# Block-sparse attention and SwiGLU: another order for GpSimd's gathers and copies in the sparse steps

## The chip, the cores and the metric

One core of one Trainium2 chip runs the whole program. The metric is device time in microseconds (us). Engines are named as the profile names them: PE (TensorE, matrix multiply), DVE (VectorE), ACT (ScalarE), POOL (GpSimd), SP (SyncE, which here only issues DMAs). Each engine executes its own instructions strictly in the order of the program and waits on semaphores for the others. DMAs started by POOL are issued by instructions that stand in POOL's own queue.

## The reference, cut to what matters

```python
batch, n_heads, seq, head_dim = (4, 8, 768, 64)      # block 32: 24 blocks of queries and of keys
scores = scale * np.matmul(q, k.transpose(0, 1, 3, 2))
mask = np.abs(blk_i - blk_j) <= 1
mask = mask | (blk_i == 0) | (blk_j == 0) | (blk_i == n_blocks - 1) | (blk_j == n_blocks - 1)
for qb in range(n_blocks):
    for kb in sampled_blocks[qb]:                    # 3 random key blocks for each query block
        mask[qb * block:(qb + 1) * block, kb * block:(kb + 1) * block] = True
attn = softmax(np.where(mask, scores, -1e9));  attn_out = np.matmul(attn, v)

x = attn_out.transpose(0, 2, 1, 3).reshape(B * S, H * D)          # 3072 tokens x 512
xn = x / np.sqrt(np.mean(x * x, axis=-1, keepdims=True) + 1e-06) * rms_g
g = xn @ w_gate                                                    # 512 x 1536
out = (g * sigmoid(g) * (xn @ w_val)) @ w_out                      # 1536 x 512
```

A query block looks at its three neighbours, the first and the last block, and three sampled blocks; the first and last query blocks look at everything.

## The kernel before, in words

**Stages.** Batch 0 is computed densely, with the mask added through extra rows of the operands (lines 926 to 1054). Batches 1 to 3 are computed sparsely, in 18 *chunks* of four query blocks (128 queries): in each batch five chunks of neighbouring blocks and one *edge* chunk (blocks 0, 23, 1, 22). In the order of work the edge chunks are numbers 5, 11 and 16. The feed-forward part (FFN) of finished tokens is cut into small pieces (`gate`, `val` and `down`, lines 730 to 786) that are fed into PE between the pieces of attention.

**Sparse steps.** The loop at line 1078 runs steps i = 0 to 18. Each step has ten *positions*. Work is put under a position with `do(n, f)`; at line 1159 the loop goes through the positions in order, runs everything put there, in the order in which it was put, and then lets `position()` add FFN pieces. This is the order of the program, hence of each engine's queue; no scheduler moves anything afterwards. Step i does the following.

- `values(i - 1, 0)` and `values(i - 1, 1)` at positions 0 and 1 (line 634): PE multiplies the probabilities of chunk i-1 with its values, 64 small matmuls for an ordinary chunk and 128 for an edge chunk (L644).
- `normalise` (L669, L670 on DVE), `squares(i - 1)` at position 4 (L677 on ACT), `rms_power(i - 1)` at position 5 (two tiny POOL instructions, L681 and L682) and `x_scaled(i - 1)` at position 7 (L698 or L695 on DVE). For most chunks the scaled rows `xs` are then transposed by a DMA that SP issues (L700) into `xg`, which the FFN reads; for chunks 4, 8, 16 and 17 (`by_pe`) PE transposes them a step later.
- `scores(i, part)` from position 1 on (L620 on PE, the exponential L628 on ACT). An ordinary chunk has four parts, an edge chunk eight.
- preparation for later chunks; nx is i + 1. The keys of chunk nx are collected in `kg` (two buffers in turn): neighbours and edges by DVE (`gather_k`, L471 and L476), sampled blocks by ACT and POOL (`sampled_k`, L485): of the three sampled blocks of a query block ACT copies two and POOL one, so POOL makes four copies for an ordinary chunk and two for an edge chunk. The values of a chunk are collected in `vg` (three buffers in turn) by indirect DMAs from a table in DRAM (`gather_v`, L512), one for each query block. An ordinary chunk has four of them, an edge chunk two, for its third and fourth block; `gather_v` skips the blocks 0 and 23, so that its call for the first two of an edge chunk issues nothing.
- keys and queries of the next batch but one are loaded (`load_kq`, L126, two POOL DMAs with a cast to bf16 on the way), values of it (`load_v`, by SP), and keys and queries of the next batch are transposed by PE (`turn`, L455) into the tables `KT` and `QN`. `table(b)` (L446) writes the table of values of a batch to DRAM, one POOL DMA, at position 0 of steps 4 and 10.

**POOL's queue around the change.** In step i the queue of POOL holds, in this order: at position 0 the copies of sampled keys of chunk nx (in step 0: at position 6); at 1 and 2 the third and fourth gather of chunk nx; at 5 `rms_power`; at 6 and 7 the first and second gather of chunk nx + 1 (at 8 and 9 where nx + 1 is the first chunk of a batch); at 9, in steps 4 to 7, `load_kq` for one pair of heads of batch 3. The variable `at` (line 1124) is 6 in step 0 and 0 in all others; it also places the copies of DVE and ACT.

Buffers bind as follows. The gathers of chunk c write `vgs[c % 3]`, which `values(c - 3)` reads last. The copies of chunk c write `kgs[c % 2]`, which `scores(c - 2)` reads last. `turn` of batch 3 reads what `load_kq` brought: keys at position 6 and queries at position 9 of steps 7 to 10. FFN groups enter at position 4 of the step two after their last chunk (line 1065): chunks 0 and 1 in step 3, chunks 2 to 4 in step 6, 5 to 8 in step 10, 9 to 12 in step 14, 13 to 15 in step 17.

Of the kernel before, what the change touches and what calls it, by code (L numbers as in the profile page):

```python
# [18 lines left out]
def kernel(  # L19
# [57 lines left out]
    PB = NCH // (B - 1)  # L77
    sizes = [2, 3, 4, 4, 3, 2]
    assert sum(sizes) == NCH
    sgroups, at = [], 0  # L80
# [384 lines left out]
    def gather_k(i, copy):  # L465
        b, qbs = chunks[i]
        kg, src = kgs[i % 2], KT[b % 2]
        j0 = 2 if qbs[0] == 0 else 0
        n = QB - j0
        step = (qbs[j0 + 1] - qbs[j0]) * HB  # L470
        yield lambda: copy(  # L471
            out=kg[:, :, j0:QB, W0:W0 + 3 * HB],
            in_=spaced(src[:, :, (qbs[j0] - 1) * HB:(qbs[j0] + 2) * HB], step, n, 3 * HB))
        if i % PB < 2:
            for to, at in ((F0, 0), (L0, NT - HB)):
                yield lambda to=to, at=at: copy(  # L476
                    out=kg[:, :, :, to:to + HB],
                    in_=src[:, :, at:at + HB].unsqueeze(2).to_broadcast([P, H, QB, HB]))

    def sampled_k(i, on):  # L480
        b, qbs = chunks[i]

        def one(j, r):
            copy = act if by_act(qbs[j], r) else pool
            copy(out=kgs[i % 2][:, :, j, R0 + r * HB:R0 + (r + 1) * HB],  # L485
                 in_=KT[b % 2][:, :, bass.ds(kat[(qbs[j], r)], HB)])

        return [lambda j=j, r=r: one(j, r) for j in range(QB) if qbs[j] not in (0, NB - 1)
                for r in range(NRND) if by_act(qbs[j], r) == (on == "act")]

    def gather_q(i, copy):
        b, qbs = chunks[i]
        runs = [(0, QB)] if qbs[0] else [(0, 2), (2, QB)]
        for lo, hi in runs:
            for a in range(2):
                for w in range(2):
                    rows = QN[b % 2][w * D:(w + 1) * D]
                    to = Qd[i % 2][a * D:(a + 1) * D, :, a, w, lo * HB:hi * HB]
                    if qbs[0]:
                        yield lambda to=to, rows=rows: copy(  # L500
                            out=to, in_=rows[:, :, qbs[0] * HB:(qbs[0] + QB) * HB])
                    else:
                        yield lambda to=to, rows=rows, lo=lo, hi=hi: copy(
                            out=to.rearrange("p h (j s) -> p h j s", j=hi - lo),
                            in_=spaced(rows[:, :, qbs[lo] * HB:(qbs[lo] + 1) * HB],
                                       (qbs[lo + 1] - qbs[lo]) * HB, hi - lo, HB))

    def gather_v(i, js=range(QB)):
        b, qbs = chunks[i]
        for j in js:  # L510
            if qbs[j] not in (0, NB - 1):
                nc.gpsimd.indirect_dma_start(  # L512
                    vgs[i % 3][:, j, :], None, vtab[b][:],
                    bass.IndirectOffsetOnAxis(ap=vidx[:, qbs[j]:qbs[j] + 1], axis=0))
# [563 lines left out]
    for i in range(NCH + 1):  # L1078
        jobs = {}

        def do(n, f):
            jobs.setdefault(n, []).append(f)
# [3 lines left out]
        nx = i + 1 if i + 1 < NCH else None  # L1086
# [36 lines left out]
        if nx is not None:  # L1123
            at = 6 if nx == 1 else 0
            gk, gq = list(gather_k(nx, dve)), list(gather_q(nx, dve))
            if at == 0:
                for m, x in enumerate(gq):
                    do(3 + m * 2 // len(gq) * 2, x)
                do(4, gk[0])
                for x in gk[1:]:  # L1130
                    do(6, x)
            else:
                do(at, gk[0])
                for m, x in enumerate(gk[1:]):
                    do(at + 1 + m, x)
                for m, x in enumerate(gq):
                    do(at + 1 + m // 2, x)
            kact, kpool = sampled_k(nx, "act"), sampled_k(nx, "pool")
            for x in kpool:
                do(at, x)  # L1140
            for m, x in enumerate(kact):
                do(at + (m + 1) * (NPOS - 1 - at) // len(kact), x)
            if nx > 1:
                do(1, lambda: gather_v(nx, (2,)))
                do(2, lambda: gather_v(nx, (3,)))
            if nx + 1 < NCH:
                at = 6 if (nx + 1) % PB else 8
                do(at, lambda: gather_v(nx + 1, (0,)))
                do(at + 1, lambda: gather_v(nx + 1, (1,)))
        for m in range(min(6, len(by_need)) if i < 2 else 0):  # L1150
            do(m, next_address)

        bl, sl = divmod(i + 2, PB)
        if 0 < bl and bl + 2 < B and sl < NP:
            do(9, lambda: load_kq(bl + 2, sl))
        bv, sv = divmod(i + 3, PB)
# [44 lines left out]
```

## Time and profile before

| what | value |
|---|---|
| time, median of 3 runs | 309.54 us (309.53 to 310.64) |
| the profiled execution's own time | 309.54 us |
| its span, first to last instruction of the program | 307.8 us |
| mean granted TensorE clock | 0.994 |
| PE busy | 284.4 us, 92% |
| DVE, ACT, POOL busy | 215.2, 198.9, 147.1 us |
| sparse steps | from about 75 us to the end |

What lies between the span and the time (1.7 us) is start and end of the execution. The views used below are the profile's page (busy time of the engines, costliest groups), the table of waits (who waited for whom, total in us, times, longest), the chain of work that ended last, and the timeline of single engines. In a timeline row the columns are the start, the duration, the engine, the line, the operation and its tiles, the count, and in brackets the idle time before it with what ended it. A wait put down to "issue" ended with nothing that the profile shows.

### The profile page before, as it was taken

To read this page: it belongs to the slowest core of one execution; us is meant where nothing else is said; L and a number is where in the kernel's file an instruction comes from. 1 tells how busy PE (TensorE), PEld (TensorE's weight loads), DVE (VectorE), ACT (ScalarE), POOL (GpSimd) and SP (SyncE) were. 2 spreads that over 40 slices of the span, in tenths; PEclk is the share of its full clock that TensorE was granted. 3 is DMA by queue.
4 is the path that set the end of the run, shared out by engine and by line. 5 is a ranking of instruction groups with operands and counts; after the bars stand their busy time and mean duration, and the time that the engine had idled before them with its cause. 6 is when DMAs were issued, how large, how long until landed. Compare 5 with 4: busy or idle time off the path is not lost.

```text
span 307.8 us, 9872 instructions
## 1 busy us (share of the span) xinstructions
PE 284.4 (92%) x3871; PEld 187.8 (61%) x3871; DVE 215.2 (70%) x596; ACT 198.9 (65%) x467; POOL 147.1 (48%) x244
## 2 busy tenths in 40 slices
PE   7899999978969889998899898899999999999995
PEld 6677885767548657765566454454445455555683
DVE  7888798667847757963999377877449991396480
ACT  4896775666738787876898786662675575633331
POOL 9858243582746364884887542816550710000000
PEclk9999999999989999999999999999999999999999
DMA  7999999999663287598997654415543233100202
GB/s 137 290 208 201 207 227 281 257 298 227 133 200 86 76 205 267 105 250 227 141 250 205 202 163 116 119 44 148 157 156 87 78 83 100 58 2 0 104 1 68
DMA packets 37426, 47.44 MB, mean 154 GB/s; under 512 B 11184, under 2 KB 29380, under 8 KB 37380
## 3 DMA queue, kind: packets, MB, share of 16 engines
q0 software_dynamic: 21184, 32.60, 48.3%
q1 hardware_dynamic: 16132, 14.18, 15.9%
q8 instruction: 30, 0.49, 0.6%
q14 instruction: 16, 0.13, 0.2%
q10 hardware_dynamic: 64, 0.03, 0.0%
HBM read 46.45 MB, written 8.83 MB: 180 GB/s over the span
## 4 chain that ended last, share of the span: by engine, by line
PE 77%; DMA 8%; DVE 5%; issue 5%; POOL 2%; ACT 1%; ACTq 0%; DVEq 0%; POOLq 0%
PE gp L737 19%; PE vp L748 19%; PE yp L766 17%; PE st L620 7%; PE op L644 6%; DMA gain<-in_moe_rms_g_dram 4%; PE st L527 3%; PE tqk L455 2%; DMA kbf<-in_k_dram 2%; DMA xg<-xs 2%; PE op L536 2%; DVE u L752 1%; DVE hps L756 1%; DVE junk L570 1%; POOL kbf L126 1%
## 5 line engine op out<-in xcount | busy, mean ns | idle before, releaser
L737 PE MATMUL gp<-xg,wg 128*128 128x256 bf16 (+2 forms) x432 | 81.6, 309 | 2.3 <-ACT yo L771 1.1
L748 PE MATMUL vp<-xg,wv 128*128 128x256 bf16 (+2 forms) x432 | 81.3, 310 | 2.1 <-DVE u L752 1.2
L741 ACT ACTIVATE th<-gp 128x256 bf16<-128x256 f32 (+2 forms) x108 | 50.0, 463 | 44.0 <-PE gp L737 30.3
L512 POOL DMA_INDIRECT vg<-vtab,vidx x66 | 66.9, 1014 | 18.2 <-issue 13.6
L766 PE MATMUL yp<-wo,hps 128*128 128x512 bf16 (+1 forms) x300 | 72.0, 371 | 0.2 <-issue 0.2
L752 DVE SCALAR_TENSOR_TENSOR u<-th,gp 128x256 bf16<-128x256 bf16 (+2 forms) x108 | 54.5, 505 | 24.4 <-ACT th L741 20.9
L628 ACT ACTIVATE ex<-st 128x512 bf16<-128x512 f32 x84 | 50.4, 600 | 31.3 <-PE st L620 29.9
L756 DVE TENSOR_TENSOR hps<-u,vp 128x256 bf16<-128x256 bf16 (+2 forms) x108 | 55.1, 510 | 18.7 <-PE vp L748 3.3
L737 PEld LDWEIGHTS <-wg 128*128 128x128 bf16 x432 | 39.6, 98 | 20.5 <-issue 3.9
L748 PEld LDWEIGHTS <-wv 128*128 128x128 bf16 x432 | 39.6, 98 | 20.3 <-issue 3.4
L681 POOL TENSOR_TENSOR ssq<-ssq,eps 128x1 f32<-128x1 f32 x18 | 3.5, 195 | 86.6 <-ACT junk L677 86.5
L766 PEld LDWEIGHTS <-hps 128*128 128x128 bf16 x300 | 26.0, 98 | 20.9 <-issue 0.5
L530 ACT ACTIVATE ex<-st 128x768 bf16<-128x768 f32 x42 | 33.3, 813 | 5.3 <-PE st L527 4.9
L644 PEld LDWEIGHTS <-ex 128*32 128x32 bf16 x1344 | 16.2, 95 | 21.8 <-issue 20.1
L644 PE MATMUL op<-vg,ex 128*32 128x66 bf16 x1056 | 20.8, 196 | 7.1 <-issue 6.8
L771 ACT ACTIVATE yo<-yp 128x512 f32<-128x512 f32 (+1 forms) x25 | 14.6, 584 | 17.1 <-PE yp L766 16.8
L527 PE MATMUL st<-wide_q,wide_k 88*128 88x256 bf16 x144 | 23.0, 272 | 1.5 <-DVE wide_q L345 1.1
L669 DVE RECIPROCAL rz<-op 128x4 f32<-128x4 f32 x36 | 6.4, 177 | 15.4 <-PE op L644 9.7
L620 PE MATMUL st<-wide_q 128*128 128x64 bf16 x256 | 16.0, 197 | 0.6 <-issue 0.6
L620 PEld LDWEIGHTS <-wide_q 128*128 128x128 bf16 x256 | 12.9, 101 | 5.6 <-issue 0.8
L527 PEld LDWEIGHTS <-wide_k 88*128 88x128 bf16 x144 | 12.9, 97 | 5.3 <-DVE wide_q L345 2.0
L670 DVE TENSOR_TENSOR stage<-op,rz 128x256 bf16<-128x256 f32 x36 | 15.3, 425 | 1.2
(147 smaller groups left out, 385.4 us busy)
## 6 DMA issues: line engine op xcount, KB each, us to landing
out_dram<-yo SPq DMA_DIRECT2D x20, 256.0 KB
vraw<-in_v_dram SPq DMA_DIRECT2D x12, 384.0 KB
kbf<-in_k_dram POOLq DMA_DIRECT2D x15, 192.0 KB
vtab<-Vs POOLq DMA_DIRECT2D x3, 792.0 KB
qbf<-in_q_dram POOLq DMA_DIRECT2D x12, 192.0 KB
vraw<-in_v_dram POOLq DMA_DIRECT2D x4, 384.0 KB
wg<-in_moe_w_gate_dram POOLq DMA_DIRECT2D x4, 384.0 KB
wv<-in_moe_w_val_dram POOLq DMA_DIRECT2D x4, 384.0 KB
```

The costliest lines, as they stand in the source:

```text
L512: nc.gpsimd.indirect_dma_start(vgs[i % 3][:, j, :], None, vtab[b][:], bass.IndirectOffsetOnAxis(ap=vidx[:, qbs[j]:qbs[j] + 1], axis=0))
L527: nc.tensor.matmul(out=at[:, e], lhsT=KT0[0:KR, h, jt * P:(jt + 1) * P], rhs=QT0[0:KR, h, c0 * P:(c0 + 2) * P], start=True, stop=True)
L530: nc.scalar.activation(out=ex[:, 3 * part:3 * (part + 1), :], in_=at[:, 0:3], func=AF.Exp, scale=SCALE)
L620: nc.tensor.matmul(out=st[:, at:at + UN], lhsT=lhsT, rhs=Qd[i % 2][:, h, :, :, j * HB:(j + 1) * HB].rearrange("p a w s -> p (a w) s"), sta ...
L628: nc.scalar.activation(out=ex.rearrange("p (u s w) -> p u s w", s=HB, w=2), in_=st.rearrange("p (u w s) -> p u s w", s=HB, w=2), func=AF.E ...
L644: nc.tensor.matmul(out=op[j * BLK:(j + 1) * BLK, at:at + VW], lhsT=lhsT, rhs=rhs, start=(n == 0), stop=(n == of - 1))
L737: nc.tensor.matmul(out=gp[:, 0:tg], lhsT=wg[:, c, f * P:(f + 1) * P], rhs=xg[:, c, 0:tg], start=(c == 0), stop=(c == KD - 1))
L741: nc.scalar.activation(out=th[:, 0:tg], in_=gp[:, 0:tg], func=AF.Tanh, scale=0.5)
L748: nc.tensor.matmul(out=vp[:, 0:tg], lhsT=wv[:, c, f * P:(f + 1) * P], rhs=xg[:, c, 0:tg], start=(c == 0), stop=(c == KD - 1))
L752: nc.vector.scalar_tensor_tensor(out=u[:, 0:tg], in0=th[:, 0:tg], scalar=1.0, in1=gp[:, 0:tg], op0=ALU.add, op1=ALU.mult)
L756: nc.vector.tensor_tensor(out=hps[f][:, 0:tg], in0=u[:, 0:tg], in1=vp[:, 0:tg], op=ALU.mult)
L766: nc.tensor.matmul(out=yp, lhsT=hps[f][:, tt * P:(tt + 1) * P], rhs=wo[:, f, lo:hi], start=(f == 0), stop=(f == NF - 1))
```

## The change

In every step the copies of sampled keys by POOL go from position 0 to position 6, behind `rms_power`. The third and fourth gather of chunk nx go from positions 1 and 2 to 0 and 1. The first and second gather of chunk nx + 1 go from 6 and 7 to 2 and 3, ahead of `rms_power`; where nx + 1 begins a batch they stay at 8 and 9. The loads of keys and queries of batch 3 go from position 9 of steps 4 to 7 to position 9 of steps 5 to 8. Number, kind and size of all instructions stay as they were, and in the built program PE, DVE, ACT and SP have the same instructions in the same order as before.

```diff
             for x in kpool:
-                do(at, x)
+                do(6, x)
             for m, x in enumerate(kact):
                 do(at + (m + 1) * (NPOS - 1 - at) // len(kact), x)
             if nx > 1:
-                do(1, lambda: gather_v(nx, (2,)))
-                do(2, lambda: gather_v(nx, (3,)))
+                do(0, lambda: gather_v(nx, (2,)))
+                do(1, lambda: gather_v(nx, (3,)))
             if nx + 1 < NCH:
-                at = 6 if (nx + 1) % PB else 8
+                at = 2 if (nx + 1) % PB else 8
                 do(at, lambda: gather_v(nx + 1, (0,)))
                 do(at + 1, lambda: gather_v(nx + 1, (1,)))
...
-        bl, sl = divmod(i + 2, PB)
+        bl, sl = divmod(i + 1, PB)
         if 0 < bl and bl + 2 < B and sl < NP:
             do(9, lambda: load_kq(bl + 2, sl))
```

## The prediction

> **What bounds the kernel now.** I read the page first (busy shares, costliest groups), then the table of waits, then the timelines of POOL, PE and ACT in the steps where POOL has most to do, then the chain that ended last. From the page:
>
> ```profile
> span 307.8 us, 9872 instructions
> PE 284.4 (92%) x3871; PEld 187.8 (61%) x3871; DVE 215.2 (70%) x596; ACT 198.9 (65%) x467; POOL 147.1 (48%) x244
> ...
> PE 77%; DMA 8%; DVE 5%; issue 5%; POOL 2%; ACT 1%; ACTq 0%; DVEq 0%; POOLq 0%
> ...
> L512 POOL DMA_INDIRECT vg<-vtab,vidx x66 | 66.9, 1014 | 18.2 <-issue 13.6
> ...
> L681 POOL TENSOR_TENSOR ssq<-ssq,eps 128x1 f32<-128x1 f32 x18 | 3.5, 195 | 86.6 <-ACT junk L677 86.5
> ```
>
> PE is busy for 284.4 of 307.8 us, so that all its idle time together is 23.4 us, start and end of the kernel included. POOL is busy for under half of the span; most of its idle time, 86.5 us, it spends in front of the RMS power, waiting for ACT's squares. The change moves work of POOL alone, so it can only matter where somebody waits for POOL or for a DMA that POOL issues. From the table of waits (engine and line, whom it waited for, total us, times, longest):
>
> ```profile
> POOL ssq L681 <- ACT junk L677: 86.5, 15, 15.4
> DVE xs L698 <- POOL rstd L682: 2.1, 2, 2.0
> PE op L644 <- issue: 8.0, 16, 1.0
> DVE xs L695 <- POOL rstd L682: 1.5, 2, 1.2
> ...
> PE gp L737 <- DMA xg<-xs: 0.8, 1, 0.8
> ```
>
> Nobody waits for POOL's copies, PE hardly ever for a gather (0.4 us in all, by the answer on L644), and DVE four times for the RMS power, 3.6 us. But POOL was late itself in none of these four: L681 began 0.08 us after ACT had finished (chunk 8: ACT's accumulator ends at 170.76, L681 starts at 170.84). What remains for PE is 0.8 us on one transpose and 8.0 us of short gaps inside the small matmuls of `values`.
>
> Now POOL's timeline in its fullest stretch, steps 7 and 8, where the loads of batch 3 come on top:
>
> ```profile
> 152.99 0.18 POOL L681 TENSOR_TENSOR ssq<-ssq,eps 128x1 f32<-128x1 f32 x1
> 153.26 0.80 POOL L682 TENSOR_TENSOR rstd<-ssq,mhalf 128x1 f32<-128x1 f32 x1
> 154.23 1.00 POOL L512 DMA_INDIRECT vg<-vtab,vidx  x1 [0.17 <-issue]
> 155.54 0.96 POOL L512 DMA_INDIRECT vg<-vtab,vidx  x1 [0.30 <-issue]
> 156.50 0.80 POOL L126 DMA_DIRECT2D kbf<-in_k_dram  x1
> 157.26 0.81 POOL L126 DMA_DIRECT2D qbf<-in_q_dram  x1
> 157.99 1.06 POOL L485 COPY wide_q<-wide_k 128x128 bf16 x4
> 159.23 1.05 POOL L512 DMA_INDIRECT vg<-vtab,vidx  x1 [0.17 <-issue]
> 160.58 1.00 POOL L512 DMA_INDIRECT vg<-vtab,vidx  x1 [0.31 <-issue]
> 161.61 0.19 POOL L681 TENSOR_TENSOR ssq<-ssq,eps 128x1 f32<-128x1 f32 x1
> ```
>
> From one RMS power to the next are 8.62 us without a wait: RMS power 1.07, two gathers 2.44, two loads 1.49, four copies 1.06, two gathers 2.56. ACT's squares came at 152.91 and 161.53, also 8.62 us apart. POOL is exactly full here, and anything put ahead of the RMS power would show.
>
> **The change part by part.** It adds and removes no instruction. I place each moved one by adding these durations to the times at which the other engines were ready in the profiled execution, whose time, 309.54 us, equals the median.
>
> *Two gathers ahead of the RMS power, and a new wait.* The first two gathers of chunk i+2 now stand at positions 2 and 3 of step i, and write the buffer that `values(i-1)` has just read. POOL waits for PE's last matmul of `values(i-1)`, and the RMS power of chunk i-1 is queued behind that. That happens in ten steps. From the end of `values` to the end of ACT's accumulator there are 3.71 us (chunk 4: 128.11 to 131.82) to 6.22 us; the two gathers take 2.44. They fit where POOL stands ready when `values` ends. Where POOL is full it comes later, and the RMS power slips. For chunk 4: RMS power of chunk 3 ends at 124.64, two copies to 125.2, six gathers to 132.9 (`values(4)` ended at 128.11, no wait), L681 at 133.0 instead of 132.27, 0.7 us late; its reader `xs` began at 134.94 and the power would end at 133.9. For chunk 6: from 145.43, copies to 146.5, loads to 148.0, gathers to 150.5 and 153.0, L681 0.1 late. Chunk 7: 0.2 late. `xs` of these two began 2.47 and 2.23 us after the power. Cost 0; with that cover gone 1.0 us in all. In front of chunk 8's power, where DVE does wait, the two gathers would belong to edge chunk 11 and do not exist.
>
> *The copies behind the RMS power.* They become ready later by most of a step, and `scores` of chunk i+1 follow. For chunk 8, PE and ACT before:
>
> ```profile
> 156.47 1.05 PE L644 MATMUL op<-vg,ex 128*32 128x66 bf16 x64
> 157.45 0.41 PE L620 MATMUL st<-Qd,kg 128*128 128x64 bf16 x8
> ...
> 156.96 0.30 ACT L485 COPY kg<-wide_k 128x128 bf16 x1
> ```
>
> POOL's copies for it ended at 150.43, 7.0 us ahead of the scores. They would now end at 155.2, 2.2 us ahead, and ACT's last copy into the same tile (156.96 plus 0.30) comes later still. Worked out alike, the cover is 3.1 us for chunk 2, 2.0 for chunk 3, 2.2 for chunk 7, 1.8 for chunk 9 and more elsewhere. Cost 0.
>
> A rule speaks against this place: the Trainium skill, "SBUF — State Buffer", section "Who interferes with whom", says that a DVE instruction with two SBUF inputs and a GpSimd one that reads SBUF exclude each other. The copies now begin where DVE begins `xs`, which at L698 has two such inputs. The trace has such a meeting: copies at 97.23 took 1.52 us instead of 1.0, `xs` at 97.26 took 0.88 instead of 0.75. In the two steps with copies where DVE waits for the power at L698 (chunks 12 and 15) this is 0.13 each by the rows, 0.3 us on an engine with idle time: 0 in the sum, 0.3 its upper end. By the rule in full, DVE held for one whole copy (0.36, L485's longest group mean), it would be at most 0.7 us.
>
> *The other gathers* come about 3 us earlier and change nothing: `vg` had landed at least 8 us before its reader (chunk 8: last landing 156.96 by its semaphore, `values` at 165.01). In step 0 the first gather of chunk 2 passes two loads for batch 2, delayed by 1.3 us and not needed before 123 us. Cost 0.
>
> *The loads of batch 3* move from 127.1, 135.7, 147.9 and 156.5 to about 134.9, 146.5, 155.2 and 164. The longest landing that the trace gives for them is 8.3 us, the transposes on PE that read them start at 153.11, 161.65, 170.08 and 180.62: at least 5 us remain. SP's queue has none of this. Cost 0; with the cover gone PE would stand until the landing, up to 8 us.
>
> *DMA traffic beside the transpose of chunk 1.* The chain of work that ended last runs through it:
>
> ```profile
> 107.48 0.67 DVE xs L698
> ...
> 108.18 5.91 DMA xg<-xs
> 114.09 0.14 issue
> 114.22 0.60 PE gp L737 x4
> ```
>
> PE waits 0.8 us for it. Before, four gathers were issued between 106.3 and 112.6; now the copies come first, and two gathers follow from about 107.5, the other pair having gone out near 99. The wait can vanish (-0.8) or, if the transpose takes as long as the longest one (6.85 us, issued at 147.96 beside loads), grow by 0.9. With half as many gathers beside it I take half of the wait: -0.4. The Trainium skill, "DMA: Bandwidth & Descriptors", section "SWDGE vs HWDGE vs iDMA", says that an engine serves the queues of the two kinds of DMA in turn; by that alone halving the other side would take the whole wait, -0.8, sum 308.7. That the one transpose with no gather near it took 2.4 us (253.93) agrees.
>
> *The gaps in `values`.* Their cause is not in the trace: "issue". Those in the sparse steps come within some 2 us of a DMA issued by POOL, and `values` of chunks 14, 16 and 17, with none, have no gap; but chunks 7 and 8 have DMAs and no gap either. After the change the gathers still fall into or just ahead of most `values`; only chunk 11's (gaps of 0.32, 0.49 and 0.46) become free of them: -1.3 if gathers are the cause. At the other end, six chunks without gaps (1, 2, 7, 8, 12, 15) might get one of 0.5 each: +3.0. I take 0, because nearly every chunk keeps its neighbours.
>
> Sum: 309.54 - 0.4 = 309.1 us.
>
> **The rivals.** *Faster.* The transpose's wait goes and chunk 11's gaps go: 309.54 - 0.8 - 1.3 = 307.4 us. For it: the gaps stand beside gathers. Against: the clean chunks with gathers. *Slower.* PE releases the buffer later than its rows say, so the gathers reach POOL only with ACT's squares and stand whole in front of the RMS power. For it: DVE's reading of chunk 5's result waited until 140.47, though `values` ended at 138.47 by the rows. Against: most of DVE's readings show no such wait. With a lateness of 2.5 us copies miss their scores at chunks 3, 7, 8 and 9 by 0.5, 0.3, 0.3 and 0.7, and DVE, held at `xs` by up to 2.5 in the steps with chunks 12 and 14, passes on some 1.2: 309.5 + 3.0 = 312.5 us. It decides from about 1.8 us of lateness, the least cover. *The change does little of what it says.* Edge chunks and chunks that begin a batch have no gathers to move ahead; this ends where my forecast does.
>
> **How the numbers follow.** About 0.5% (1.5 us) can be told from no change. Within it 0.50: every step has a named cover of at least 1.0 us. Faster rival 0.26. Slower rival 0.24: the covers of copies shrink everywhere, and that of scores is 1.8 us at the least. The likeliest case gives 309.1, alone 307.9 to 311.0. The range goes from 306.9 (the faster rival with half a microsecond of gaps more) to 312.4, nearly the slower rival.
>
> **What would show it.** Right: L681 within 0.8 us of ACT's accumulator in each step; no wait of PE on POOL's copies before `scores`; POOL waiting for PE before gathers where it waited for ACT. Wrong: DVE waiting more than 3.6 us for L682; PE standing at L620 for L485 or at L455 for loads; the gaps at L644 far from 8.0 us.

## The result, and the profile after

The changed kernel takes 325.79 us (median of 6 runs, 324.20 to 326.87) beside 310.05 us of the kernel before (6 runs, 308.99 to 311.59): 1.0516 times as long, 95% interval 1.0478 to 1.0554. The forecast was 309.1 us, with a range up to 312.4. The kernel before itself takes 308.99 to 311.59 us in some sets of runs (a set is made on one chip) and 290.20 to 292.39 us in others, and the result above is from a set of the first kind. I call them *sets with gaps* and *sets without gaps*, for the reason that the trace gives.

The profiled execution of the changed kernel took 326.87 us. From its page:

```profile
span 325.1 us, 9900 instructions
...
PE 293.6 (90%) x3871; PEld 192.8 (59%) x3871; DVE 215.6 (66%) x596; ACT 199.9 (61%) x467; POOL 145.4 (45%) x244
...
PEclk9999999999979999599987999989999999999999
...
L512 POOL DMA_INDIRECT vg<-vtab,vidx x66 | 66.0, 1000 | 28.3 <-issue 12.2
...
L644 PE MATMUL op<-vg,ex 128*32 128x66 bf16 x1056 | 23.3, 197 | 15.0 <-issue 14.6
```

And from its table of waits (engine and line, whom it waited for, total us, times, longest):

```profile
POOL ssq L681 <- ACT junk L677: 89.3, 16, 15.4
...
PE op L644 <- issue: 15.8, 30, 1.2
...
POOL vg L512 <- PE op L644: 9.9, 8, 3.0
...
DVE xs L698 <- POOL rstd L682: 3.8, 2, 3.3
...
DVE xs L695 <- POOL rstd L682: 2.1, 2, 1.8
```

The span grew by 17.3 us (307.8 to 325.1). PE's busy time grew by 9.2 (284.4 to 293.6) and its idle time, span less busy, by 8.1 (23.4 to 31.5). Two readings fill this.

*Idle.* The gaps inside `values` (L644 by "issue") went from 8.0 us in 16 places to 15.8 in 30: 7.8 of the 8.1. Chunk 4 shows what one looks like. PE, with the matmuls of both halves of `values(4)` and the FFN between them:

```profile
127.15 0.43 PE L644 MATMUL op<-vg,ex 128*32 128x66 bf16 x32
127.51 0.73 PE L748 MATMUL vp<-xg,wv 128*128 128x256 bf16 x4
128.50 0.24 PE L644 MATMUL op<-vg,ex 128*32 128x66 bf16 x4 [0.26 <-ACT th L741]
129.21 0.26 PE L644 MATMUL op<-vg,ex 128*32 128x66 bf16 x4 [0.47 <-issue]
130.12 0.25 PE L644 MATMUL op<-vg,ex 128*32 128x66 bf16 x3 [0.66 <-issue]
130.87 0.21 PE L644 MATMUL op<-vg,ex 128*32 128x66 bf16 x2 [0.50 <-issue]
131.57 0.25 PE L644 MATMUL op<-vg,ex 128*32 128x66 bf16 x3 [0.49 <-issue]
132.28 0.43 PE L644 MATMUL op<-vg,ex 128*32 128x66 bf16 x16 [0.45 <-issue]
```

POOL in the same stretch:

```profile
126.45 1.07 POOL L512 DMA_INDIRECT vg<-vtab,vidx  x1 [0.16 <-PE vp L748]
127.83 0.95 POOL L512 DMA_INDIRECT vg<-vtab,vidx  x1 [0.31 <-issue]
129.08 0.95 POOL L512 DMA_INDIRECT vg<-vtab,vidx  x1 [0.30 <-issue]
130.34 0.95 POOL L512 DMA_INDIRECT vg<-vtab,vidx  x1 [0.30 <-issue]
132.97 0.95 POOL L512 DMA_INDIRECT vg<-vtab,vidx  x1 [1.68 <-PE op L644]
```

The rows of the first half take 0.43 us for its 32 matmuls. The second, with the same work, takes from 128.50 to 132.71: two to four matmuls, then a gap of about half a microsecond, five times. Three gathers are issued meanwhile. In the kernel before this half took 0.84 us (from 127.27).

The end of a matmul in such a row is modelled, so a row shows what PE was given and not when the result was there. That is seen at DVE, which needs `vp` (L748); by PE's row that is finished at 128.24:

```profile
132.46 0.42 DVE L756 TENSOR_TENSOR hps<-u,vp 128x256 bf16<-128x256 bf16 x1 [2.71 <-remote]
```

"Remote" means that the semaphore update that ended the wait fits the end of no instruction. PE's updates due at 127.58 (the end of the first half) and at 128.24 (`vp`) are recorded at 132.38 and 132.44. What PE had been given before the gaps was late by more than four microseconds, too.

*Busy.* The granted clock, stretch by stretch around this place (start and end, length, PE's busy time, clock, share of the DMA engines, GB/s):

```profile
120.00:131.00 11.00, 8.17 (x148) 1.00 0.76 165
131.20:137.90 6.70, 5.88 (x68) 0.50 0.82 238
138.00:144.00 6.00, 5.29 (x103) 1.00 0.53 84
```

Right behind the gaps PE runs at half clock. The records of the granted clock have 0.500 from 131.16 for 6.83 us and four times for 3.41 us (from 90.20, 161.88, 172.12 and 216.49). In the 3.41 us ahead of each, PE was busy for 1.2 to 1.9 us. Four of the five come behind gaps in `values`. The one from 161.88 does not: there PE stood by "issue" for 1.19 us at scores (L620, until 160.38) and 0.74 us at an FFN piece (L748, until 161.80), beside a row of four gathers (155.97 to 160.84). The trace of before has one such stretch, 3.41 us from 89.79. That is 20.47 against 3.41 us. PE was busy for 19.2 and 3.4 us of them, so that half clock took about 7.9 us more, most of the 9.2 by which PE's busy time grew. The Trainium skill, "TensorE: Matmul & The Clock Gate", section "Part 1: The HAM clock gate (the "warmup" mystery)", says that a monitor halves the clock by how busy PE was in a window of some 3.4 us; stretches of 3.41 us and twice that, at exactly half, agree with it.

### The profile page after: what moved, and what is told of

The parts are those of the page before. It is cut to its first block, busy times and chain, and to the rows that moved or that the text cites. A ratio compares the mean times of both kernels' runs of the same rounds, so it can differ in the third digit from the quotient of the medians.

```text
span 325.1 us, 9900 instructions
## 1 busy us (share of the span) xinstructions
PE 293.6 (90%) x3871; PEld 192.8 (59%) x3871; DVE 215.6 (66%) x596; ACT 199.9 (61%) x467; POOL 145.4 (45%) x244
## 2 busy tenths in 40 slices
DMA packets 37427, 47.44 MB, mean 146 GB/s; under 512 B 11185, under 2 KB 29381, under 8 KB 37381
## 4 chain that ended last, share of the span: by engine, by line
PE 76%; issue 7%; DMA 6%; DVE 5%; POOL 3%; ACT 1%; DVEq 0%; ACTq 0%; POOLq 0%
PE gp L737 19%; PE vp L748 19%; PE yp L766 18%; PE st L620 8%; PE op L644 7%; DMA gain<-in_moe_rms_g_dram 4%; DMA qbf<-in_q_dram 2%; PE tqk L455 2%; PE st L527 1%; PE op L536 1%; DVE u L752 1%; DVE hps L756 1%; DVE junk L570 1%; POOL kbf L126 1%; POOL q L119 1%
## 5 line engine op out<-in xcount | busy, mean ns | idle before, releaser
L737 PE MATMUL gp<-xg,wg 128*128 128x256 bf16 (+2 forms) x432 | 84.8, 318 | 1.5 <-issue 0.8
L748 PE MATMUL vp<-xg,wv 128*128 128x256 bf16 (+2 forms) x432 | 83.7, 317 | 2.1 <-issue 1.0
L512 POOL DMA_INDIRECT vg<-vtab,vidx x66 | 66.0, 1000 | 28.3 <-issue 12.2
L737 PEld LDWEIGHTS <-wg 128*128 128x128 bf16 x432 | 40.7, 100 | 21.7 <-issue 5.3
L748 PEld LDWEIGHTS <-wv 128*128 128x128 bf16 x432 | 40.2, 100 | 20.4 <-issue 3.7
L681 POOL TENSOR_TENSOR ssq<-ssq,eps 128x1 f32<-128x1 f32 x18 | 3.9, 216 | 94.9 <-ACT junk L677 89.3
L644 PE MATMUL op<-vg,ex 128*32 128x66 bf16 x1056 | 23.3, 197 | 15.0 <-issue 14.6
L644 PEld LDWEIGHTS <-ex 128*32 128x32 bf16 x1344 | 17.7, 96 | 31.2 <-issue 29.6
L620 PE MATMUL st<-wide_q 128*128 128x64 bf16 x256 | 16.6, 199 | 1.7 <-issue 1.7
L669 DVE RECIPROCAL rz<-op 128x4 f32<-128x4 f32 x36 | 6.4, 177 | 17.3 <-PE op L644 8.6
L620 PEld LDWEIGHTS <-wide_q 128*128 128x128 bf16 x256 | 13.2, 102 | 6.2 <-issue 1.2
L620 PEld LDWEIGHTS <-kg 128*128 128x128 bf16 x272 | 12.9, 100 | 5.1 <-issue 0.9
```

Of the source, the lines that this page charges most:

```text
L512: nc.gpsimd.indirect_dma_start(vgs[i % 3][:, j, :], None, vtab[b][:], bass.IndirectOffsetOnAxis(ap=vidx[:, qbs[j]:qbs[j] + 1], axis=0))
L620: nc.tensor.matmul(out=st[:, at:at + UN], lhsT=lhsT, rhs=Qd[i % 2][:, h, :, :, j * HB:(j + 1) * HB].rearrange("p a w s -> p (a w) s"), sta ...
L644: nc.tensor.matmul(out=op[j * BLK:(j + 1) * BLK, at:at + VW], lhsT=lhsT, rhs=rhs, start=(n == 0), stop=(n == of - 1))
L737: nc.tensor.matmul(out=gp[:, 0:tg], lhsT=wg[:, c, f * P:(f + 1) * P], rhs=xg[:, c, 0:tg], start=(c == 0), stop=(c == KD - 1))
L748: nc.tensor.matmul(out=vp[:, 0:tg], lhsT=wv[:, c, f * P:(f + 1) * P], rhs=xg[:, c, 0:tg], start=(c == 0), stop=(c == KD - 1))
```

## The experiments

Several explanations were set against each other. **G**: what costs time is that POOL issues indirect gathers while the small matmuls of `values` run; the order only decides how much of that happens. Against it **C** (the copies in their new place), **L** (the late loads) and **T** (the gathers' traffic).

### Undoing one part of the change each

First the gathers back behind the RMS power, the rest as changed:

```diff
-                at = 2 if (nx + 1) % PB else 8
+                at = 6 if (nx + 1) % PB else 8
```

> The changed kernel with its first part undone: the first and second gather go back behind the RMS power (positions 6 and 7); copies and loads stay as changed. Theory G (the time is lost because POOL issues indirect gathers while PE runs the many small matmuls of values; PE then has gaps inside them, 15.8 us instead of 8.0, and its clock falls to half for 20.5 us instead of 3.4): the gathers stand about where they stood before, so the gaps come back to 8 to 11 us, the half clock to under 8 us, the time to 309 to 316 us. Theory C (the copies of sampled keys behind the RMS power cost the time): it stays at 322 to 327. Theory L (the later loads of batch 3 cost it): it stays at 322 to 327.

Measured: 335.07 us (333.79 and 336.34), beside 310.41 of the kernel before; ratio 1.0804, 1.0696 to 1.0911. A miss for G as I had put it: worse than the whole change. Its gaps at L644 are 46, together 24.0 us. The trace says why: the copies stand directly ahead of the first two gathers, and the third and fourth follow at once at the start of the next step. All four go out in one row that ends inside the next `values`. Ahead of or behind the RMS power is not what counts.

Then the copies back at position 0:

```diff
-                do(6, x)
+                do(at, x)
```

> The changed kernel with its second part undone: POOL's copies of sampled keys go back to position 0, gathers ahead of the RMS power and late loads stay. Theory G: the third and fourth gather come one copy group (1.06 us) later in the step, so still into values; 318 to 327 us, gaps at values 12 to 17 us. Theory C: 309 to 312 us. Theory L: 322 to 327 us.

Measured: 318.43 and 324.53 us; 19 gaps, 8.9 us, in the profiled one (the shorter). The times are those of theory G and not the 309 to 312 of theory C, but the gaps are fewer than the 12 to 17 us that G had said: in this trace PE stands by "issue" for another 7.5 us at other lines. And the loads back:

```diff
-        bl, sl = divmod(i + 1, PB)
+        bl, sl = divmod(i + 2, PB)
```

> The changed kernel with its third part undone: keys and queries of batch 3 are loaded a step earlier again. Theory G: steps 4 to 8 keep their gathers beside values, 320 to 328 us, gaps 13 to 17 us. Theory C: 322 to 327 us. Theory L: 309 to 313 us.

Measured: 324.70 us (324.23 and 325.17), ratio 1.0469 (1.0413 to 1.0526), and the same 20.47 us of half clock. The late loads cost nothing that these runs can tell; L falls.

### The same bytes, plainly

In the changed kernel each indirect gather becomes a plain DMA, by POOL and at the same place, of the same 128 rows of 4,224 bytes. The choice of rows is left out: the rows come from fixed places.

```diff
-                nc.gpsimd.indirect_dma_start(
-                    vgs[i % 3][:, j, :], None, vtab[b][:],
-                    bass.IndirectOffsetOnAxis(ap=vidx[:, qbs[j]:qbs[j] + 1], axis=0))
+                nc.gpsimd.dma_start(
+                    out=vgs[i % 3][:, j, :], in_=vtab[b][8 * j:8 * j + P, :])
```

> The changed kernel, with each indirect gather replaced by a plain DMA from POOL that brings as many rows of the same length (128 of 4224 bytes) from fixed rows of the same table, to the same buffer at the same place in the queue; the choice of the value rows by index is left out. If the indirect issue is what disturbs PE (theory G in its narrow form): the gaps at values fall under 4 us, no half clock inside the work, 300 to 310 us. If the bytes that come in beside values disturb PE (theory T, traffic): gaps stay at 12 to 17 us and the time at 320 to 327.

Measured: **290.22 us** (290.20 and 290.25), ratio 0.9358 (0.9319 to 0.9397), in the set in which before took 310.41; that is 10 us less than even theory G had said. From its page (line numbers are one lower behind L512):

```profile
PE 278.0 (96%) x3871; PEld 184.9 (64%) x3871; DVE 214.8 (74%) x596; ACT 199.1 (69%) x467; POOL 114.9 (40%) x244
...
PEclk9999999999999999999999999999999999999999
...
L512 POOL DMA_DIRECT2D vg<-vtab x66 | 36.2, 557 | 18.0 <-PE op L643 14.4
...
L643 PE MATMUL op<-vg,ex 128*32 128x66 bf16 x1056 | 16.6, 195 | 0.0
```

Not one gap at the line of `values` (0.0 us idle), and no half clock before the last microseconds, with the copies, the loads and the traffic where the change puts them. C, L and T fall in this set. What is left is what the two kinds of gather differ in: the indirect issue, its length on POOL (1.00 us each against 0.56) and the rows that are read. The 290.22 suggests that it costs the kernel before, too, some 20 of its 310.41 us; plain gathers in the order of before were not run in a set with gaps.

### The same in another set of runs

Next the converse (plain gathers in the order of before), the gathers alone and the copies alone moved, and indirect gathers of only the 48 sampled rows, with the other 80 rows, whose place is known, brought by three plain DMAs of SP:

```diff
                 nc.gpsimd.indirect_dma_start(
-                    vgs[i % 3][:, j, :], None, vtab[b][:],
-                    bass.IndirectOffsetOnAxis(ap=vidx[:, qbs[j]:qbs[j] + 1], axis=0))
+                    vgs[i % 3][R0:F0, j, :], None, vtab[b][:],
+                    bass.IndirectOffsetOnAxis(ap=vidx[R0:F0, qbs[j]:qbs[j] + 1], axis=0))
+                for lo, hi, at in ((F0, W0, NT if qbs[j] == 1 else 0),
+                                   (W0, L0, (qbs[j] - 1) * HB),
+                                   (L0, P, NT if qbs[j] == NB - 2 else NT - HB)):
+                    nc.sync.dma_start(out=vgs[i % 3][lo:hi, j, :],
+                                      in_=vtab[b][at:at + hi - lo, :])
```

> The order of before, with each indirect gather replaced by a plain DMA of POOL that moves the same 128 rows of 4,224 bytes from fixed places (the choice of rows is left out). Theory G (what disturbs the tensor engine is that POOL issues an indirect gather while the short matmuls of `values` run; the order only decides how much of the issuing falls there): about 290 us, as the order of after gave with plain gathers, 290.2, no gaps of 0.48 us at the attention-by-values line and no stretch of half clock behind them; the whole difference between the two orders vanishes. Theory O (the order of after costs something besides: copies too late, loads too late, waits): 290 minus 15.7, that is about 275 us, or at least some microseconds under 290.2.

> Before, with the gathers alone moved (first and second at 2 and 3, third and fourth at 0 and 1); copies and loads stay. Theory G: most of the loss is here: 319 to 323 us, half clock 10 us or more, gaps at the attention-by-values line over 11 us. Theory C (the copies behind the RMS power cost by themselves, in POOL's port or in waits): the gathers alone give at most a third of the loss, 310 to 315 us.

> Before, with POOL's copies alone moved behind the RMS power; gathers and loads stay. Theory G: the copies do not disturb the tensor engine; they only shift the gathers by about 1 us (third and fourth earlier, first and second later), so the result goes by how the gathers fall then: within 5 us of 310.4, and the gaps at the attention-by-values line follow the gathers' overlap with it. Theory C: 315 us or more with the gaps beside the copies themselves.

> The order of before; each indirect gather fetches only the 48 sampled rows, and the 80 rows whose place is known beforehand come by three plain DMAs of SP (16, 48 and 16 rows). Same bytes, same number of indirect gathers, full computation. Theory R (the disturbance goes with the rows that an indirect gather addresses): gaps and half clock shrink to about 3/8 of the 20 us that plain gathers saved: about 297 us. Theory I (it goes with the issue as such, whatever its rows): about 310 us, or more by SP's 198 further DMAs.

Measured: nothing that decides, since the kernel before took 291.16 us here (25 runs, 290.44 to 292.39). Plain gathers 292.13 (1.0037, 1.0006 to 1.0067), gathers alone 292.12 (1.0032, 1.0017 to 1.0047), copies alone 290.76 (0.9985, 0.9970 to 1.0001), fewer rows 295.22 (1.0153, 1.0129 to 1.0177; PE waits 3.6 us for two transposes that SP issues). The indirect gathers are there as before and take as long, 1005 ns each with the copies moved, but no trace of this set has gaps: at most 0.2 us at the line of `values`. So the changed kernel itself was run once more, and with it a kernel with two gathers behind `values` and two behind the RMS power:

```diff
             for x in kpool:
                 do(at, x)
...
-            if nx > 1:
-                do(1, lambda: gather_v(nx, (2,)))
-                do(2, lambda: gather_v(nx, (3,)))
             if nx + 1 < NCH:
-                at = 6 if (nx + 1) % PB else 8
+                at = 2 if (nx + 1) % PB else 6
                 do(at, lambda: gather_v(nx + 1, (0,)))
                 do(at + 1, lambda: gather_v(nx + 1, (1,)))
+                do(max(6, at + 2), lambda: gather_v(nx + 1, (2,)))
+                do(max(7, at + 3), lambda: gather_v(nx + 1, (3,)))
```

> The changed kernel once more, since the kernel before took 310.4 us beside the first four experiments and 291.2 us beside the next four, where not one gap of 0.48 us stood at the attention-by-values line. Theory P (the disturbance of the short matmuls by indirect gathers belongs to some chips): where the kernel before takes about 310 us, the changed one takes about 325 and has some 15 us of gaps and 20 us of half clock; where it takes about 291, the changed one has no such gaps and takes 291 to 293, by the sums of the prediction (0 for the loads, 0 to 1 for the copies, 1 for POOL's lateness, which reached 3.25 us in front of the RMS power when the gathers alone were moved). Theory Q (the order as such costs the 5%): a ratio of 1.05 on either.

> Before, with the four gathers of a chunk issued one after the other behind `values` (positions 2, 3 and behind the RMS power 6, 7), so that as few as possible run beside a `values`; copies and loads as before. Under theory P, where the kernel before takes 310: 300 to 308 us, fewer gaps than its 8.0 us; where it takes 291: no gaps, 290 to 293 us, since POOL's order is then hidden but for its lateness. Under theory Q (some other cost of gathers that stand ahead of the RMS power): slower than before on either, 300 or more beside 291.

Measured, again in a set without gaps (before 290.82, 9 runs): the changed kernel **292.40** us (6 runs, 291.32 to 294.29), ratio **1.0055, 1.0023 to 1.0087**; two and two 296.53 (1.0202, 1.0176 to 1.0229), above the 290 to 293 expected. The order as such does not cost 5%. It costs 1.6 us. PE's longest wait in its sparse steps is this one:

```profile
PE gp L737 <- DMA xg<-xs: 1.4, 1, 1.4
```

and in the chain of work that ended last:

```profile
99.72 0.66 DVE xs L698
...
100.42 6.51 DMA xg<-xs
106.92 0.14 issue
107.06 0.60 PE gp L737 x4
```

This is the transpose of chunk 1, for which the kernel before waited 0.8 us in the prediction's trace. With the gathers alone moved PE does not wait for it, though there, too, two gathers were issued beside it (at 99.38 and 100.72, in the changed kernel at 98.75 and 100.09). So I can't say that the order alone makes it late, and since the kernel before was not traced in a set without gaps, the 1.6 us can't be put down to single waits.

### The parts, in a set with gaps

> The kernel before itself, for a trace of it beside the following runs. Theory P (the disturbance belongs to some chips or times, and is there for a whole series of runs): either about 310 us with some 8 us of gaps at the attention-by-values line, or about 291 us with none; the records of gathers (66 issues of about 1.0 us each) are alike in both. Theory Q (the gaps belong to the kernel's order): about 310 us with its 8 us of gaps whatever the series.

> Before, with the gathers alone moved, once more. Theory P: if the kernel before takes about 310 here, 318 to 326, most of the loss of the whole change; if it takes about 291, 292 as in the first series, POOL late in front of the RMS power by some 3 us for chunks 0 and 4 and no gaps. Theory C (the copies cause the loss where there is one): 310 to 313 beside 310.

> Before, with POOL's copies alone moved behind the RMS power, once more. Theory P: if the kernel before takes about 310 here, within 8 us of it, by how the shifted gathers meet `values`; if about 291, within 1 us of it. Theory C: 318 or more beside 310.

> Indirect gathers of 48 instead of 128 rows, the other rows by plain DMAs of SP, once more. If the kernel before takes about 310 here: theory R (the disturbance goes with the rows addressed) 297 to 302, theory I (it goes with each indirect issue) 310 to 316. If about 291: 293 to 296 as in the first series, where PE waited 3.6 us for two transposes queued behind SP's further DMAs.

This set had gaps: before 310.60 (310.58 to 311.18), and the kernel before, traced, 309.69 with 17 gaps. Gathers alone: 322.75 (1.0385, 1.0343 to 1.0427). Copies alone: **333.61** (1.0734, 1.0694 to 1.0775). Fewer rows: 315.01 and 323.63. So the copies alone are worse than the whole change, in a kernel that takes 290.76 elsewhere. That is a miss for theory P (within 8 us of before) and the number that theory C had named (318 or more). But the copies by themselves are not it: with plain gathers they stand in the same place, in a set with gaps, and PE has no gap. The copies alone are the best pair to look at, since nothing but the set differs. The second half of `values(0)` with the copies moved, PE and POOL, in the set without gaps:

```profile
81.02 0.95 POOL L512 DMA_INDIRECT vg<-vtab,vidx  x1 [0.30 <-issue]
...
82.20 0.43 PE L644 MATMUL op<-vg,ex 128*32 128x66 bf16 x32
82.27 0.94 POOL L512 DMA_INDIRECT vg<-vtab,vidx  x1 [0.30 <-issue]
```

and in the set with gaps:

```profile
84.11 0.21 PE L644 MATMUL op<-vg,ex 128*32 128x66 bf16 x2
84.18 0.95 POOL L512 DMA_INDIRECT vg<-vtab,vidx  x1 [0.30 <-issue]
84.53 0.23 PE L644 MATMUL op<-vg,ex 128*32 128x66 bf16 x3 [0.21 <-issue]
85.43 0.95 POOL L512 DMA_INDIRECT vg<-vtab,vidx  x1 [0.30 <-issue]
85.93 0.24 PE L644 MATMUL op<-vg,ex 128*32 128x66 bf16 x4 [1.18 <-issue]
86.67 0.19 PE L644 MATMUL op<-vg,ex 128*32 128x66 bf16 x1 [0.50 <-issue]
86.69 0.95 POOL L512 DMA_INDIRECT vg<-vtab,vidx  x1 [0.30 <-issue]
87.37 0.23 PE L644 MATMUL op<-vg,ex 128*32 128x66 bf16 x3 [0.51 <-issue]
88.08 0.22 PE L644 MATMUL op<-vg,ex 128*32 128x66 bf16 x1 [0.48 <-issue]
88.80 0.46 PE L644 MATMUL op<-vg,ex 128*32 128x66 bf16 x18 [0.50 <-issue]
88.94 0.42 DVE L756 TENSOR_TENSOR hps<-u,vp 128x256 bf16<-128x256 bf16 x1 [4.25 <-remote]
89.00 0.38 ACT L741 ACTIVATE th<-gp 128x256 bf16<-128x256 f32 x1 [4.04 <-remote]
```

The gather is issued as fast in both (0.94 and 0.95 us); PE's same 32 matmuls take 0.43 us in one and from 84.11 to 89.26 in the other, and come back to speed about a microsecond after the last gather of the row has been issued. DVE and ACT stand for over 4 us, too: they wait for `vp` and `gp`, which PE was given ahead of these matmuls (from 83.13 and 83.58). In the set without gaps the same two start at 82.89 and 82.95. The row is there because of the copies' place: behind the RMS power they stand ahead of the first two gathers, the third and fourth follow at once, and the row of four runs into the next `values`, as with the gathers put back in the first experiment.

The table puts the traces beside each other. Worked out from each timeline: every stretch of L644 (half a `values`, or both halves where nothing stands between), the time of L512 that falls into it, and the idle time of PE at L644 over 0.1 us. Half clock leaves the last microseconds of the execution out; in five of the traces (before again, copies back, gathers alone, loads back, gathers back) 3.41 us of it lie at 67 to 69 us, ahead of the sparse steps.

| kernel (profiled execution) | time | gather issue inside `values` | gaps at `values` | half clock |
|---|---|---|---|---|
| **sets with gaps** | | | | |
| before | 309.54 | 11.8 | 17, 8.1 us | 3.41 |
| before again | 309.69 | 12.2 | 17, 7.2 | 10.24 |
| fewer rows (48 of 128) | 315.01 | 13.0 | 22, 9.6 | 3.41 |
| changed, copies back | 318.43 | 13.4 | 19, 8.9 | 10.23 |
| gathers alone | 322.32 | 14.0 | 22, 10.3 | 13.65 |
| changed, loads back | 325.17 | 16.4 | 29, 13.7 | 20.47 |
| changed | 326.87 | 19.3 | 32, 16.2 | 20.47 |
| copies alone | 333.22 | 26.2 | 46, 20.9 | 23.88 |
| changed, gathers back | 333.79 | 27.2 | 46, 24.0 | 23.88 |
| changed, plain gathers | 290.20 | 3.7 (plain) | 0 | 0 |
| **sets without gaps** | | | | |
| changed again | 292.41 | 6.3 | 0 | 0 |
| gathers alone | 292.01 | 5.9 | 0 | 0 |
| copies alone | 290.56 | 9.7 | 1, 0.2 | 0 |
| fewer rows (48 of 128) | 293.04 | 6.1 | 0 | 0 |

In the sets with gaps the time goes with the third column through nine traces. The column is partly its own effect, since a `values` that stands still has more gathers issued beside it. But the traces without gaps give the meeting as the order alone makes it: 5.9 for the gathers alone, 6.3 for the change, 9.7 for the copies alone, the order in which they stand where there are gaps (322.75, 325.79, 333.61). The fewer rows, with 6.1 and 315.01 or 323.63 us, do not fit this order. With 48 instead of 128 rows in each gather the gaps did not shrink (9.6 us against 8.1 and 7.2), against the expectation of 3/8; they go with the issue and not with the rows, as far as one trace and two times that differ by 8.6 us can tell.

`values` shows the gaps best, but it is not alone. In the nine traces with indirect gathers in sets with gaps, PE stands by "issue" at other lines as well, for 2.8 to 7.5 us in all (before 4.2, changed 4.3), and every wait by "issue" over 0.1 us, from 56 us on, lies within 1 us of the issue of a gather. The first such place is ahead of the sparse steps: behind the first row of four gathers (61.41 to 66.27 in before) PE resumes its transposes (L455) after 1.4 to 2.8 us in all nine, and after 0.6 us in every other trace.

### Gathers beside no `values`

Last, the kernel before with all four gathers directly behind the `values` that frees their buffer:

```diff
-            if nx > 1:
-                do(1, lambda: gather_v(nx, (2,)))
-                do(2, lambda: gather_v(nx, (3,)))
             if nx + 1 < NCH:
-                at = 6 if (nx + 1) % PB else 8
-                do(at, lambda: gather_v(nx + 1, (0,)))
-                do(at + 1, lambda: gather_v(nx + 1, (1,)))
+                at = 2 if (nx + 1) % PB else 8
+                do(at, lambda: gather_v(nx + 1))
```

> Before, with all four gathers of a chunk in one row directly behind the `values` that frees their buffer, ahead of the RMS power (but for the chunks that begin a batch); copies and loads as before. They take about 5 us from the end of one `values`, and the next begins 7 us or more later, so that hardly any runs beside one; the RMS power comes 1 to 3 us late. Theory G (gaps where an indirect gather is issued beside `values`), if the kernel before takes about 310 here: gaps under 3 us, little half clock, 293 to 300 us; if it takes about 291: 293 to 297, the lateness alone. Theory S (where the gaps occur they slow any order with gathers, wherever they are put): 308 or more beside 310.

> Two gathers behind `values` and two behind the RMS power, once more. Theory G, if the kernel before takes about 310 here: by how many of the last two still run when the next `values` begins: 298 to 308, less than before, more than with all four directly behind `values`. If about 291: 296.5 as before, with POOL 7 us late in front of the RMS power of chunk 4. Theory S: 308 or more beside 310.

> All four gathers directly behind `values`, once more, since the last series had no gaps in the kernel before (290.95). If it takes about 310 here: theory G 297 to 304 (297.6 by the lateness alone, as just measured, and what gaps are left in the chunks that begin a batch), under 3 us of gaps at the attention-by-values line; theory S 315 or more. If about 291: 297.6 again.

> All four gathers directly behind `values`, a third time, for a series in which the kernel before takes about 310. There theory G: 297 to 304 and under 3 us of gaps at the attention-by-values line; theory S: 315 or more. If the kernel before takes about 291: about 297 again, and the question stays open.

Measured: all three sets in which this was run had no gaps (before 290.95, 291.14 and 291.09). All four behind `values` took 297.60 (1.0229, 1.0199 to 1.0259), 296.76 (1.0195) and 297.62 (1.0225); two and two, in the first of them, 294.90 (1.0136, 1.0060 to 1.0213) instead of the 296.5 expected. Whether this order leaves out the gaps where there are any stays open. What the runs do give is the price of a late POOL, the prediction's slower rival, without gaps. POOL from the second of the three:

```profile
87.68 0.98 POOL L512 DMA_INDIRECT vg<-vtab,vidx  x1 [0.16 <-PE tqk L455]
...
91.48 0.95 POOL L512 DMA_INDIRECT vg<-vtab,vidx  x1 [0.30 <-issue]
92.45 0.20 POOL L681 TENSOR_TENSOR ssq<-ssq,eps 128x1 f32<-128x1 f32 x1
```

ACT's accumulator for chunk 0 had ended at 87.07. Behind four gathers the RMS power is 5.4 us late, and 5.2 us for chunk 4 (124.79 and 129.95). DVE waits 9.1 us for it (6.8 and 2.3 us, in six places) and the kernel loses 5.6 to 6.7 us; two of the three traces have 3.41 and 6.83 us of half clock besides, near 95 us. With the gathers alone moved the lateness is 3.1 and 3.25 us for these two chunks, and the loss 1.0 us.

## Why the prediction was wrong

**The step that failed** is the one on the gaps in `values`, taken as 0 with ends of -1.3 and +3.0 us, "because nearly every chunk keeps its neighbours". The gaps grew by 7.8 us, and PE's work took about 7.9 us longer at half clock, most of it behind them. It went wrong in three ways. I counted neighbours (is there a gather near this `values`?) where the length of the row counts: before, a pair of gathers stood between the RMS power and the copies, and another pair behind these; changed, four follow one another and PE stands until they are through. The upper end was made of six new gaps of 0.5 us, though the trace of before had a stretch with 2.47 us of gaps, chunk 0's second half (85.18 to 88.97, gather issue for 60% of it):

```profile
86.44 0.36 PE L644 MATMUL op<-vg,ex 128*32 128x66 bf16 x18 [1.04 <-issue]
87.29 0.27 PE L644 MATMUL op<-vg,ex 128*32 128x66 bf16 x5 [0.49 <-issue]
88.01 0.28 PE L644 MATMUL op<-vg,ex 128*32 128x66 bf16 x5 [0.46 <-issue]
88.78 0.19 PE L644 MATMUL op<-vg,ex 128*32 128x66 bf16 x1 [0.48 <-issue]
```

Six chunks of that size would have made the upper end +14.8. And the clock was not in the sum at all: the row PEclk of before had one 8 among its nines, behind just this stretch (half clock from 89.79).

```profile
PEclk9999999999989999999999999999999999999999
```

A second look at it would have shown that these 2.47 us of gaps were followed by 3.41 us at half clock, which is 1.7 us of work more.

**The remark on clean chunks** ("chunks 7 and 8 have DMAs and no gap either") was right and pointed to the answer: what is issued beside those two is a load and copies; the issue of indirect gathers takes 2% and 5% of these stretches. I had put all DMAs of POOL into one class. Chunk 14 was not without: a gather's issue ends at 231.31, 0.9 us ahead of its `values`.

**Two gathers ahead of the RMS power** (0; lateness up to 0.7 us): in the predicted trace L681 starts 0.08 or 0.09 us behind ACT's accumulator in all 18 chunks, and POOL waits for PE instead, 9.9 us in eight places. The forecast was met, but by luck: PE had become slower. Without gaps the RMS power is 2.29 us late for chunk 0 and 1.55 for chunk 4; chunk 0 I had not looked at.

**The copies behind it** (0): no wait of PE for them in either trace. The least cover was not 1.8 us, as I had it, but 0.8 (chunk 14: copies end at 237.97, scores start at 238.78), and without gaps none at all for chunk 2 (91.48 and 91.46). The rule of the Trainium skill ("SBUF — State Buffer", section "Who interferes with whom") would have held DVE for a whole copy, 0.36 us; where the two meet in the changed kernel without gaps, four copies took 1.45 us (from 90.03) and `xs` 0.83 instead of 0.75 (from 90.50), so that 0 to 0.3 was the right size.

**The loads** (0): right, by 324.70 with them put back.

**The transpose of chunk 1** (-0.4, ends -0.8 and +0.9): PE's wait is gone in the predicted trace, and 1.4 us in the set without gaps, 0.6 more than the 0.8 of before in a set with gaps: inside the ends, but of the other sign. That the one transpose with no gather near it took 2.4 us said little: the ones issued at 98.20, 165.53 and 210.55, with a gather's issue within 1 us, had moved their last packet after 2.1 to 2.4 us.

**The rivals.** The faster one did not come. The slower one, a late POOL, is real but was not what decided: in a set without gaps the changed kernel shows a part of it, and loses 1.6 us, beside the wait of 1.4 above. Without gaps the sum of -0.4 stands against +1.6 (0.7 to 2.5 by the interval).

**What stays open.** That the indirect gathers, and not their bytes or the copies, make PE stand in sets with gaps is shown by the plain gathers (no gap, 290.22 beside 310.41) and the traces above. That it is the issue as such and not its length on POOL is not shown: a plain issue takes 0.56 us instead of 1.00, so that plain gathers also meet `values` for less time (3.7 us). How an issue on POOL holds PE back is not shown either: the profile names no releaser. PE does not wait for its own instructions there: in the set with gaps no packet of the instruction queues runs between 84.11 and 89.26, where the copies alone have their gaps (the nearest begin at 81.4 and 93.2).

One rival was left untested. All these times were taken with the profiler on, and its own records suffer at the same places. DVE and ACT make 877 semaphore updates in each of these kernels. The nine traces with gaps lack 59 to 133 of their records, all within 1.3 us of the issue of a gather; the other traces lack 0 to 16, and those with plain gathers none. So taking the trace may be part of what holds PE back, and whether the gaps are there without it is not known; a run with the profiler off would tell.

Nor is it known what distinguishes the two kinds of sets: with the gathers alone moved (without gaps) and in before (with gaps), the pages have the same DMA packets (37426, 47.44 MB) and gathers of about the same length (996 and 1014 ns). The recorded number of the chip was 6 for two sets with gaps and also for one without, and other numbers for four without, so that it may be the chip, the moment or something that no record holds. Whether gathers kept away from `values` help in a set with gaps was not seen.

## What to carry to other kernels

A gap by "issue" that only shows beside one kind of instruction of another engine is a cost of that meeting. Before that engine's queue is reordered, add up how long such instructions stand in a row, and take the worst stretch of the trace, not the typical one, as the price of a meeting. See in the rows of the engines that wait for PE, not only in PE's own, when its results were there. Look at the granted clock at the same time: here a PE that was busy for half of three microseconds went on at half clock. And time an order in more than one set of runs before it is kept: here the same edit is 5.2% or 0.5% slower, and the copies alone 7.3% slower or not at all.

## What the hardware showed that I had not expected

- The issue of an indirect gather by POOL (about 1.0 us each) brought PE's small matmuls, in some sets of runs, down to one to four in some 0.72 us, and held up PE's other matmuls and its signals to DVE and ACT as well (4.25 us of waiting in the stretch shown); plain DMAs of the same bytes from the same place of the queue did not (0.56 us each, no gap).
- Half clock comes in stretches of 3.41 us and twice that behind such places: 3.41 and 10.24 us in all in two traces of before, 20.47 in the changed kernel, up to 23.88 us. PE need not stand still for it: in the changed kernel it was busy for 1.2 to 1.9 of the 3.41 us ahead.
- The same kernel differs by 6.6% between sets of runs, 291.16 and 310.41 us, with a mean granted clock of 0.998 to 1.0 in the one and 0.982 to 0.994 in the other. With plain in place of indirect gathers the changed kernel takes 290.22 us beside the 310.41.
